# Fewer, larger loads of q and k for the first and the last batch of a fused attention and adapter kernel

## The chip, the cores and the metric

The kernel runs on one core of a Trainium2 chip. The metric is the device time of one execution in microseconds; the median of the runs is given. Times inside the kernel come from the profile of one execution and count from the start of its span.

## The reference

Four batches of 6400 rows of 256 columns. Attention here is between columns (a 256 x 256 matrix for each batch), and its output goes through a mixture of adapters, two of eight for each row.

```python
qn = q / (np.linalg.norm(q, axis=1, keepdims=True) + 1e-06)
kn = k / (np.linalg.norm(k, axis=1, keepdims=True) + 1e-06)
s = kn.transpose(0, 2, 1) @ qn / tau          # per batch 256 x 256, summed over all 6400 rows
s = s - s.max(-1, keepdims=True)
a = np.exp(s); a /= a.sum(-1, keepdims=True) + 1e-09
x = (v @ a).reshape(B * N, 256)
...
logits = x @ w_gate                            # 8 experts, the two largest
for e in range(E):                             # rows that chose e, with their softmax weight w
    z = x[mask] @ A[e]                         # 256 x 16
    delta[mask] += w[mask, k, None] * (z @ B[e])
return x + delta
```

All inputs and the output are float32. q, k, v and the output are 26.2 MB each.

## The kernel before

Each batch is cut into 50 chunks; a chunk of q, k or v is 128 rows of 256 columns, one row on each partition, and a row of the file lies so that consecutive chunks are consecutive in memory for a partition. One chunk is 128 KB in float32 and is turned into bf16 by the load itself. A load of n chunks is therefore 128 runs of n KB.

q and k of a batch go to one buffer, `qk`, of 50 chunks each. There is only one, so a chunk of the next batch may be written only after the same chunk of this batch has been read by PE (`gram`, L259, and `norm`, L270 or L276) and by the engine that squares it (`square`, L251 on ACT, L253 on DVE). v has two buffers, each for one of the three pieces of a batch; v of the last batch goes to `qk`, which is free by then.

For a batch, `gram` adds k^T q over the 50 chunks in PSUM, and `norm` adds the squares through a matrix of ones. The chain of small steps `chain0` to `chain6` makes the softmax and the products with the gate and with A. After that the chunks of v are taken in pairs, one pair to a slot of a long software pipeline: transposes on PE (L409), gate logits for a group of five pairs (L431), z (L517), its transpose (L541), y (L533 and L553), and a copy of the finished pair to the ring `ys` (L557). Batch 0 is read by a loop of its own, two chunks a turn, with squares on DVE and ACT in turn. It runs as far as the loads let it. Batches 1 to 3 are spread over the slots by `GRAM`: batch 1 in slots 8 to 22, batch 2 in 26 to 46, batch 3 in 50 to 68; slot s carries pair s of v.

The stores of finished groups are put off (`DEFER`, `send`): the first goes out late, several groups are sent as one later on, and the last ones are small and issued by SP (L561).

All loads but the first stand in one list, `LOADS`, and are issued by POOL in that order. "q1.13-26" is q of batch 1, chunks 13 to 25. `load_more` is called at each turn of the loop and at each slot: it issues from the list until it comes to a piece whose place in the buffer is still to be read by instructions not yet written. The chunks 0 to 3 of batch 0 are loaded by SP in float32 and cast by DVE and ACT. The three calls `load_more(6)`, `load_more(2)` and `load_more(5)` at the start set how many pieces go out ahead of the constants that POOL makes (`ident`, `ident_f`). The same list order is then the order in which the pieces stand in the queue; an issue waits on POOL for its buffer, and all that stand behind it in the list wait with it.

Of the kernel before, what the change touches and what calls it, by code (L numbers as in the profile page):

```python
# [16 lines left out]
def kernel(  # L17
# [30 lines left out]
    VB, YB = 2, 10  # L48

    VP = [[18, 16, 16]] * 3 + [[26, 24]]  # L50
    LOADS = """q0.4-13 k0.4-13 q0.13-26 k0.13-26 q0.26-38 k0.26-38 q0.38-50 k0.38-50 v0.0-18
        q1.0-13 k1.0-13 v0.18-34 q1.13-26 k1.13-26 q1.26-50 k1.26-38 v0.34-50 k1.38-50
        q2.0-13 k2.0-13 v1.0-18 q2.13-32 k2.13-32 v1.18-34 q2.32-50 k2.32-50 v1.34-50
        q3.0-19 k3.0-19 v2.0-18 q3.19-38 k3.19-38 v2.18-34 q3.38-50 k3.38-50 v2.34-50
        v3.0-26 v3.26-50"""
    SPLIT = {(1, 1): (15, 100, 7), (1, 2): (7, 108, 13)}
    ENDS = 4
# [43 lines left out]
    loads = []  # L101
    for x in LOADS.split():
        c0, c1 = x[3:].split("-")
# [7 lines left out]
    def v_piece(b, c):  # L111
        s = 0
        while c >= VP[b][s]:
            c -= VP[b][s]
            s += 1
        return s, c
# [7 lines left out]
    def load_by_rows(dst, src, m, parts):  # L124

        nc.gpsimd.dma_start(dst[:, ENDS:m - ENDS, :], src[:, ENDS:m - ENDS, :])
        r = 0
        for n in parts:
            nc.gpsimd.dma_start(two_ends(dst, m)[r:r + n], two_ends(src, m)[r:r + n])
            r += n  # L130
        if r < P:
            for c in (0, m - ENDS):
                nc.gpsimd.dma_start(dst[r:P, c:c + ENDS, :], src[r:P, c:c + ENDS, :])

    def load_more(limit=1000):

        while limit and at_load[0] < len(loads):
            kind, b, c0, c1 = loads[at_load[0]]
            if kind in "qk":
                if b > 0 and done[b - 1] < c1:  # L140
                    return
                w, src = (0, q_v) if kind == "q" else (1, k_v)
                nc.gpsimd.dma_start(qk[:, w, c0:c1, :], src[b, :, c0:c1, :])  # L143
            else:
                s, _ = v_piece(b, c0)
                if b == B - 1:

                    if done[b] < c1 or now[0] < HOLD.get(s, 0):
                        return
                    t = qk[:, 0, c0:c1, :]  # L150
                    if s in HOLD:

                        nc.gpsimd.tensor_copy(t[0:1, 0, 0:1], pr[now[0] - 1]["vT"][0:1, 0, 0, 0:1])
                else:
                    n = len(left)
                    if n >= VB and left[n - VB]:
                        return
                    left.append(c1 - c0)
                    t = v_pool.tile([P, max(VP[0]), C], BF16, tag="v", name="vt")[:, 0:c1 - c0, :]
                tiles[b, s] = t  # L160
                if (b, s) in SPLIT:
                    load_by_rows(t, v_v[b, :, c0:c1, :], c1 - c0, SPLIT[b, s])
                else:
                    nc.gpsimd.dma_start(t, v_v[b, :, c0:c1, :])
            at_load[0] += 1
            limit -= 1
# [13 lines left out]

    DL = E * C // P
    nc.sync.dma_start(ast, moe_A.rearrange("e (h l) r -> (e h) (l r)", l=DL))
    load_more(6)
    ones_bf = const.tile([P, P], BF16)
    nc.vector.memset(ones_bf, 1.0)
    ones_f = const.tile([P, P], FP32)
# [3 lines left out]
    for c in range(0, FIRST, 2):  # L190
        nc.vector.tensor_copy(qk[:, 0, c:c + 2, :], stage[:, 0, c:c + 2, :])
        nc.scalar.copy(qk[:, 1, c:c + 2, :], stage[:, 1, c:c + 2, :])
    load_more(2)
    ident = const.tile([P, P], BF16)
    make_identity(nc, ident)
    ident_f = const.tile([P, P], FP32)
# [531 lines left out]
```

## Time and profile before

| | |
|---|---|
| median of 3 runs | 254.01 us (253.96 to 254.12) |
| profiled execution | 254.09 us, its span 252.3 us |
| granted TensorE clock, mean | 0.970 |
| busy share: PE, PE weight loads, DVE, ACT, POOL | 87%, 76%, 61%, 70%, 11% |
| moved to and from HBM | 78.91 MB read, 26.21 MB written, 417 GB/s over the span |
| packets on POOL's queue | 6368, 38.80 MB as written in bf16 |

The busy shares are means over a span with several stages. The stores are issued between 157.8 and 245.8 us; until then the DMA engines carry loads alone. The time from a load's issue to its landing, which the profile gives for each form of load, holds the wait behind the loads ahead of it.

### The profile page before, as it was taken

What the parts mean: (1) busy time and instruction counts of PE and PEld (TensorE: products, weight loads), DVE (VectorE), ACT (ScalarE), POOL (GpSimd) and SP (SyncE); (2) the same over time, 40 slices, a digit from 0 to 9 for tenths busy, and PEclk for the clock granted to TensorE, in tenths of its full rate; (3) what the DMA queues carried; (4) which work ended last, traced back from release to release, by engine and by line L of the source; (5) the groups of instructions that cost most, each with busy time, mean ns of one, the idle gap of its engine ahead of it and who ended that gap; (6) DMA issues with size and microseconds to landing.
All of it is one profiled execution on the core that took longest, in us unless ns stands there. A gap on an engine that the chain in (4) does not pass through costs nothing.

```text
span 252.3 us, 7396 instructions
## 1 busy us (share of the span) xinstructions
PE 219.3 (87%) x3122; PEld 190.8 (76%) x3122; DVE 154.8 (61%) x580; ACT 177.1 (70%) x294; POOL 27.0 (11%) x55
## 2 busy tenths in 40 slices
PE   0478769569999999999999999999999799999980
PEld 0235545347899988989999889899998699999960
DVE  2216513665657578766776877858577767877840
ACT  3315532665798979788888798798878568877870
POOL 8202101010102014105020020010001000000000
PEclk9999989997999999999999999999999899999996
DMA  7999999999999999999999999999999999999996
GB/s 215 220 221 216 217 218 214 212 213 232 203 218 214 214 222 218 203 221 209 212 219 220 216 214 214 257 272 281 269 285 427 303 308 433 411 439 410 424 417 260
DMA packets 9857, 66.80 MB, mean 265 GB/s; under 512 B 1504, under 2 KB 1760, under 8 KB 5856
## 3 DMA queue, kind: packets, MB, share of 16 engines
q0 software_dynamic: 6368, 38.80, 74.2%
q10 hardware_dynamic: 1872, 23.59, 22.2%
q1 hardware_dynamic: 1584, 3.94, 4.3%
q8 instruction: 24, 0.39, 0.6%
q14 instruction: 9, 0.07, 0.1%
HBM read 78.91 MB, written 26.21 MB: 417 GB/s over the span
## 4 chain that ended last, share of the span: by engine, by line
PE 54%; DMA 34%; DVE 5%; ACT 1%; issue 1%; POOL 1%; DVEq 0%; ACTq 0%; POOLq 0%
DMA qk<-in_k_dram 34%; PE y_ps L533 15%; PE acc L259 9%; PE zg L517 7%; PE y_ps L553 7%; PE vT_ps L409 6%; PE zg L541 4%; PE nrm L276 3%; PE vT_ps L431 3%; POOL qk L143 1%; DVE gz L521 1%; ACT sq L251 1%; DVE lg L455 0%; PE nrm L318 0%; ACT ys L557 0%
## 5 line engine op out<-in xcount | busy, mean ns | idle before, releaser
L251 ACT ACTIVATE sq<-qk 128x1024 bf16<-128x1024 bf16 x87 | 89.6, 1055 | 23.4 <-DMA qk<-in_k_dram 16.3
L259 PE MATMUL acc<-qk 128*128 128x256 bf16 x400 | 73.3, 284 | 16.4 <-DMA qk<-in_k_dram 10.1
L557 ACT COPY ys<-y_ps 128x512 f32<-128x512 f32 x100 | 58.7, 587 | 18.2 <-PE y_ps L553 16.4
L533 PE MATMUL y_ps<-ae,vT 128*128 128x256 bf16 x400 | 60.3, 273 | 0.0
L259 PEld LDWEIGHTS <-qk 128*128 128x128 bf16 x400 | 33.9, 101 | 26.7 <-DMA qk<-in_k_dram 12.0
L521 DVE TENSOR_TENSOR gz<-zg,gate 128x256 bf16<-128x256 f32 x100 | 41.7, 418 | 14.3 <-PE zg L517 12.7
L276 PEld LDWEIGHTS <-sq 128*128 128x128 bf16 x600 | 35.9, 97 | 7.6 <-ACT sq L251 4.0
L517 PE MATMUL zg<-wa_sb,vT 128*128 128x128 bf16 x400 | 38.8, 220 | 1.2 <-DVE gzT L547 1.2
L420 DVE COPY vT<-vT_ps 128x512 bf16<-128x512 bf16 x60 | 25.4, 423 | 22.5 <-PE vT_ps L409 21.3
L553 PE MATMUL y_ps<-ball_sb,gzT 128*128 128x256 bf16 x200 | 38.4, 274 | 0.0
L276 PE MATMUL nrm<-ones_bf,sq 128*128 128x1 bf16 x600 | 35.5, 164 | 2.4 <-ACT sq L251 2.1
L533 PEld LDWEIGHTS <-vT 128*128 128x128 bf16 x400 | 33.5, 97 | 2.6
L418 ACT COPY vT<-vT_ps 128x512 bf16<-128x512 bf16 x40 | 23.5, 587 | 13.2 <-PE vT_ps L409 11.7
L409 PE MATMUL vT_ps<-ident,vt 128*128 128x128 bf16 x300 | 29.0, 220 | 1.8 <-DVE vT L420 1.5
L517 PEld LDWEIGHTS <-vT 128*128 128x128 bf16 x400 | 26.5, 98 | 3.3 <-issue 1.9
L541 PE MATMUL zg<-ident,gz 128*128 128x128 bf16 x200 | 27.8, 221 | 1.2 <-DVE gz L521 0.8
L409 PEld LDWEIGHTS <-vt 128*128 128x128 bf16 x300 | 22.5, 98 | 4.1 <-issue 2.0
L547 DVE COPY gzT<-zg 128x256 bf16<-128x256 bf16 x90 | 25.2, 280 | 0.0
L253 DVE TENSOR_TENSOR sq<-qk 128x1024 bf16<-128x1024 bf16 x13 | 9.0, 692 | 23.9 <-DMA qk<-in_k_dram 15.9
L541 PEld LDWEIGHTS <-gz 128*128 128x128 bf16 x200 | 15.1, 98 | 2.7 <-DVE gz L521 2.4
L553 PEld LDWEIGHTS <-gzT 128*128 128x128 bf16 x200 | 16.2, 98 | 0.4
L270 PE MATMUL nrm<-sq,ones_bf 128*128 128x512 bf16 x50 | 16.4, 419 | 0.0
(77 smaller groups left out, 189.2 us busy)
## 6 DMA issues: line engine op xcount, KB each, us to landing
out_dram<-ys ACTq DMA_DIRECT2D x9, 1280.0 KB, 13.0
out_dram<-ys ACTq DMA_DIRECT2D x3, 2560.0 KB, 19.4
vt<-in_v_dram POOLq DMA_DIRECT2D x4, 1024.0 KB, 21.0
qk<-in_k_dram POOLq DMA_DIRECT2D x5, 768.0 KB, 28.1
out_dram<-ys ACTq DMA_DIRECT2D x1, 3840.0 KB, 22.8
qk<-in_q_dram POOLq DMA_DIRECT2D x3, 1216.0 KB, 20.1
qk<-in_k_dram POOLq DMA_DIRECT2D x3, 1216.0 KB, 25.4
vt<-in_v_dram POOLq DMA_DIRECT2D x3, 1152.0 KB, 18.2
```

The costliest lines, as they stand in the source:

```text
L251: nc.scalar.activation(sq, src, ACT.Square)
L259: nc.tensor.matmul(acc[b][:, ic, :], qk[:, 1, c, ic * P:(ic + 1) * P], qk[:, 0, c, :], start=(c == 0 and ic == 0), stop=(c == NC - 1), ski ...
L276: nc.tensor.matmul(nrm[b][:, j:j + 1], sq[:, w, c % 2, ic * P:(ic + 1) * P], ones_bf[:, 0:1], start=(c == 0 and j == 0), stop=(c == NC - 1 ...
L409: nc.tensor.matmul(pt[:, ic, sc * P:(sc + 1) * P], vt[:, o + sc, ic * P:(ic + 1) * P], ident, is_transpose=True, start=(i == 0), stop=(i = ...
L420: nc.vector.tensor_copy(dst, src)
L517: nc.tensor.matmul(z[:, sc, :], r["vT"][:, ic, sc, :], st[b]["wa"][:, ic, E:E + ER], start=(sc == 0 and ic == 0), stop=(sc == 1 and ic == ...
L521: nc.vector.tensor_tensor(out=gz.rearrange("p c (e r) -> p c e r", e=E), in0=z.rearrange("p c (e r) -> p c e r", e=E), in1=gr["gate"][:, r ...
L533: nc.tensor.matmul(y[:, sc, :], r["vT"][:, ic, sc, :], st[b]["a"][:, ic, :], start=(sc == 0 and ic == 0), stop=False, skip_group_check=True)
L541: nc.tensor.matmul(gt[:, sc, :], r["gz"][:, sc, :], ident, is_transpose=True, start=(sc == 0), stop=(sc == 1))
L547: nc.vector.tensor_copy(gzT, gt)
L553: nc.tensor.matmul(r["y"][:, sc, :], r["gzT"][:, sc, :], ball_sb, start=False, stop=(sc == 1), skip_group_check=True)
L557: nc.scalar.copy(gr["ys"][:, r["w"]:r["w"] + 2, :], r["y"])
```

## The change

Two lines of `LOADS` change, and two of the limits at the start.

Batch 0: q and k came in four pieces each (chunks 4 to 12, 13 to 25, 26 to 37, 38 to 49), q and k in turn. Now q comes in two (4 to 25, 26 to 49) and k in three (4 to 25, 26 to 36, 37 to 49). The first call issues four pieces where it issued six, the second one where it issued two; so the constants on POOL still follow the whole of batch 0's list.

Batch 3: q and k came in three pieces of 19, 19 and 12 chunks. Now q comes in two of 19 and 31, and k in three of 19, 15 and 16. The places of v's pieces between them stay: one after the first q and k, one after the second, one after the last k.

```diff
-    LOADS = """q0.4-13 k0.4-13 q0.13-26 k0.13-26 q0.26-38 k0.26-38 q0.38-50 k0.38-50 v0.0-18
+    LOADS = """q0.4-26 k0.4-26 q0.26-50 k0.26-37 k0.37-50 v0.0-18
         q1.0-13 k1.0-13 v0.18-34 q1.13-26 k1.13-26 q1.26-50 k1.26-38 v0.34-50 k1.38-50
         q2.0-13 k2.0-13 v1.0-18 q2.13-32 k2.13-32 v1.18-34 q2.32-50 k2.32-50 v1.34-50
-        q3.0-19 k3.0-19 v2.0-18 q3.19-38 k3.19-38 v2.18-34 q3.38-50 k3.38-50 v2.34-50
+        q3.0-19 k3.0-19 v2.0-18 q3.19-50 k3.19-34 v2.18-34 k3.34-50 v2.34-50
         v3.0-26 v3.26-50"""
...
-    load_more(6)
+    load_more(4)
...
-    load_more(2)
+    load_more(1)
```

## The prediction

> **What bounds the kernel now.** I read the page's slices first, then the chain, then the queue of loads row by row.
>
> ```profile
> DMA  7999999999999999999999999999999999999996
> ...
> PE 54%; DMA 34%; DVE 5%; ACT 1%; issue 1%; POOL 1%; DVEq 0%; ACTq 0%; POOLq 0%
> ```
>
> The two lines seem to disagree. The chain gives PE over half of the span, but the chain follows one last instruction back; it does not say what else was full. The slices do: the 16 DMA engines are busy in 38 of 40 slices at nine tenths or more, loads first and stores after. The kernel must move all of q, k, v and the output, and there is no slice in which the transfers wait for the compute. So I take DMA work as the bound of the whole span, and PE as a second chain that has to stay ahead of its due times. Two places show how they hang together:
>
> ```profile
> 27.48 34.30 DMA qk<-in_k_dram
> 61.88 1.06 ACT sq L251
> ...
> 78.89 27.81 DMA qk<-in_k_dram
> ```
>
> These are steps of the chain: start, length. A load of batch 1 issued at 27.48 lands at 61.78, one of batch 2 issued at 78.89 lands at 106.70. Some 30 us between issue and landing is queue, not transfer: the loads stand in line. Compute waits there for bytes, so whatever PE loses earlier is given back at these points, as long as the line itself never runs empty.
>
> At the end of the span the same question is how much the last store has to spare:
>
> ```profile
> out_dram<-ys SPq DMA_DIRECT2D x3, 256.0 KB, 5.6
> ...
> ys<-in_q_dram SPq DMA_DIRECT2D x1, 512.0 KB, 3.6
> ```
>
> The last stores of 256 KB take 5.6 us from issue to landing; at the start, with empty queues, a transfer of twice the size from the same issuer took 3.6 us. So at least 2.0 us of the 5.6 is line. PE could finish 2 us later and the last byte would land when it does now.
>
> **What a load costs besides its bytes.** The change takes out three loads in batch 0 (eight to five) and one in batch 3 (six q and k pieces to five), with the same bytes. Four issues in a row give the price, since each lands when the one ahead of it has landed and its own bytes have passed:
>
> ```profile
> 42.67 0.53 POOL L143 DMA_DIRECT2D qk<-in_q_dram  x1 [14.66 <-PE acc L259]
> 43.19 0.54 POOL L143 DMA_DIRECT2D qk<-in_k_dram  x1
> 52.70 0.53 POOL L164 DMA_DIRECT2D vt<-in_v_dram  x1 [8.98 <-PE vT_ps L409]
> 53.22 0.54 POOL L143 DMA_DIRECT2D qk<-in_k_dram  x1
> ```
>
> ```profile
> qk<-in_q_dram POOLq DMA_DIRECT2D x1, 1536.0 KB, 26.4
> qk<-in_k_dram POOLq DMA_DIRECT2D x2, 768.0 KB, 28.8
> vt<-in_v_dram POOLq DMA_DIRECT2D x1, 1024.0 KB, 24.9
> ```
>
> The second fence is of the DMA issues in that stretch, with KB each and time to landing. The 24 chunks of q (1536 KB) land at 42.67 + 26.4 = 69.07, which is 7.29 after the 61.78 above. The 16 chunks of v land at 77.60. The two 12-chunk loads of k, by their median 28.8, land in the mean at (43.19 + 53.22) / 2 + 28.8 = 77.0, and the loads ahead of them in the mean at (69.07 + 77.60) / 2 = 73.34, so a 12-chunk load takes 3.67. The slope is (7.29 - 3.67) / 12 = 0.302 us per chunk, and 3.67 - 12 x 0.302 = 0.05 us is left for the load itself. The rows are rounded to 0.1 us, so the bounds are 0 and 0.1. Four loads fewer: 0 to 0.4 us of DMA work, and I take 4 x 0.05 = 0.2 us, all of it on the bound.
>
> The Trainium skill says otherwise: "DMA: Bandwidth & Descriptors", section "Anatomy of one DMA — SWDGE (gpsimd) path", puts a fixed part of about 2.0 us on each DMA of this kind, so four loads would be worth 8 us. Here the trace disagrees for loads that stand in line: the next one's bytes flow while the fixed part passes, and 0.05 us is what is left.
>
> The POOL time of the four issues (0.53 to 0.54 each, rows above) is worth nothing: POOL waits 14.66 us ahead of one of them.
>
> **Batch 0: a later start.** Chunks 4 to 12 now come with chunk 25, not ahead.
>
> ```profile
> 19.93 0.39 PE L259 MATMUL acc<-qk 128*128 128x256 bf16 x2 [2.72 <-DMA qk<-in_k_dram]
> 20.16 0.59 PE L270 MATMUL nrm<-sq,ones_bf 128*128 128x512 bf16 x2
> 20.59 0.60 PE L259 MATMUL acc<-qk 128*128 128x256 bf16 x4
> 21.03 0.59 PE L270 MATMUL nrm<-sq,ones_bf 128*128 128x512 bf16 x2
> ...
> 35.51 0.92 PE L259 MATMUL acc<-qk 128*128 128x256 bf16 x4 [1.99 <-DMA qk<-in_k_dram]
> ...
> 41.97 1.46 PE L270 MATMUL nrm<-sq,ones_bf 128*128 128x512 bf16 x6
> ```
>
> ```profile
> 53.45 5.77 ACT L251 ACTIVATE sq<-qk 128x1024 bf16<-128x1024 bf16 x6
> ...
> 158.28 2.00 ACT L251 ACTIVATE sq<-qk 128x1024 bf16<-128x1024 bf16 x2
> ...
> 173.11 1.99 ACT L251 ACTIVATE sq<-qk 128x1024 bf16<-128x1024 bf16 x2
> ```
>
> In the first fence (PE in order of time) the waits end with landings: k's chunks up to 25 are there at 19.9, the last ones at 35.5. The same bytes stand ahead of both in the new order, so these two instants stay. A pair of chunks takes 20.16 to 21.03 = 0.87 us. The last run, 12 chunks from 35.51, took until 43.43: less six pairs (5.2) and the four closing norms (two pairs' worth, 0.87) that leaves 1.8 us, the price of starting after an idle stretch.
>
> New: chunks 4 to 25 are 11 pairs from 19.9, 9.6 us and 1.8 for the start, to 31.3. Chunks 26 to 36 have landed by then: 19.9 + 35 x 0.302 = 30.5. Five pairs to 35.6, and now PE meets the last piece at 35.5 without a gap, so the 1.8 isn't paid again. Seven pairs, 6.1, the sixteen matmuls for moe_A, which ran in the old gap (16 x 128 columns, a pair has 4 x 256 + 2 x 512, so 0.87), and the closing norms, 0.87: 43.4. Batch 0 ends where it ended. It may be a microsecond off either way, and that is covered: ACT's first six squares of batch 1 end at 59.22, and their successor waits until 61.88 for bytes, 2.7 us. Without that cover it would cost what it is late.
>
> The queue does not run empty meanwhile: q of batch 1 may follow once chunk 13 is read, about five pairs and the 1.8 after 19.9, near 26; batch 0's loads last until 35.5.
>
> **Batch 3: fewer, later.** q's second piece now reaches to chunk 50 and overwrites the last chunk of batch 2, so POOL's issue waits for PE's last gram of it, where it had gone out at 131; k's second piece queues behind it.
>
> ```profile
> 131.60 0.56 POOL L143 DMA_DIRECT2D qk<-in_k_dram  x1
> 145.23 0.53 POOL L164 DMA_DIRECT2D vt<-in_v_dram  x1 [13.07 <-PE y_ps L553]
> 145.75 0.55 POOL L143 DMA_DIRECT2D qk<-in_q_dram  x1
> 146.27 0.56 POOL L143 DMA_DIRECT2D qk<-in_k_dram  x1
> ```
>
> ```profile
> qk<-in_k_dram POOLq DMA_DIRECT2D x1, 1216.0 KB, 25.4
> ...
> qk<-in_k_dram POOLq DMA_DIRECT2D x1, 768.0 KB, 26.8
> ```
>
> ```profile
> 140.38 0.38 PE L259 MATMUL acc<-qk 128*128 128x256 bf16 x2
> ...
> 167.36 0.39 PE L409 MATMUL vT_ps<-ident,vt 128*128 128x128 bf16 x4
> ```
>
> Old: k's chunks 19 to 37 land at 131.60 + 25.4 = 157.0, the 38 chunks of the two second pieces took 38 x 0.302 + 0.1 = 11.6, so v's piece ahead of them was through at 145.4. New: q's 31 chunks can go out at 140.38 + 0.38 = 140.8, 4.6 us before that. POOL sits in that wait; behind it stand k's second piece, at once, and v's load, which goes out at 145.23 as before because its buffer is free then.
>
> Due times: k's second piece ends after 46 chunks, 145.4 + 46 x 0.302 + 0.1 = 159.4. Its first reader is the square of chunks 18 and 19, the second of the two at 158.28, so at 159.3: level. v's middle piece follows, 16 chunks: 164.3 if alone; at the mean pace from 157.0 to 173.07 (146.27 + 26.8; 40 chunks, 0.40 each, stores between them) 157.0 + 24 x 0.40 = 166.6. It is first read at 167.36: on time by 0.8 to 3. k's last piece ends with the same byte as before, 173.1; chunk 34 is squared at 174.1, the second of the two at 173.11. On time by 1. A miss of some tenths at any of the three falls into the 2.0 us of the end. Cost: 0.
>
> **Sum.** The profiled execution took 254.09 us, the span 252.3 and 1.8 around it. 254.09 - 0.2 = 253.9; the median is 0.08 below the profiled run, so 253.8.
>
> **Rivals.** Faster, by a latency that does not hide: SP's first load took 3.6 us, of which its four chunks' bytes are 1.2, so 2.4 us is latency at both ends. If each load held the queue for that long, four fewer would give 254.0 - 9.6 = 244.4. (By the price that the Trainium skill's "DMA: Bandwidth & Descriptors" gives, 246.0.) The four landings above speak against it; 2 in 100. A smaller gain of that sort, beyond 0.5 us, would need over 0.12 us per load, just above the bound; 12 in 100.
>
> Slower, by a hole in the queue: between 131 and 140.8 POOL has nothing to issue. If q's late piece arrives after v's bytes are through, the engines stand idle and DMA work, the bound, moves back one for one. With SP's 2.4 us of latency, bytes issued for at 140.8 flow by 143.2 at the latest; v's last ones, landing at 145.4, have passed by 145.4 - 2.4 = 143.0 at the earliest. Against it: even these worst ends leave a hole of 0.2 us. For it: no row shows a POOL load entering an empty queue. The point from which it decides is a latency of 2.7 us (143.0 + 0.5 - 140.8); one of 3.4, a microsecond above the row, gives up to 253.8 + 1.0 = 254.8. 20 in 100.
>
> Slower, by PE: the start in batch 0 costs over 2.7 us more than worked out, or the three due times of batch 3 are missed by more than 2.0 us together. 255, for a miss of 3; 5 in 100.
>
> No effect at all, because the 0.05 us is rounding: 254.0. It goes with the forecast; together 61 in 100.
>
> **Numbers.** About 0.2% (0.5 us) is what a measurement of this kernel can tell from no change. Forecast and no effect, 253.6 to 254.1, are within it: 0.61. Faster 0.02 + 0.12 = 0.14. Slower 0.20 + 0.05 = 0.25. The range reaches from a gain of 0.7 (the 0.4 bound and 0.3 of run scatter and doubt) to the hole's 254.8 and 0.1 of scatter: 253.3 to 254.9.
>
> **What would show it.** Right: DMA slices full as before; PE idle from 8 to 20 and then without a gap until about 43.4; the wait at 61.9 still there; the landing at 106.7 earlier by 0.1 to 0.2; q's late piece issued near 140.8, no dip in the DMA share from 142 to 145; the squares near 159.3 and 174.1 without a wait of a microsecond. Wrong: a dip there, batch 0 ending past 46, a store at the end that lands in under 4 us (the end is then PE's), or a chunk that takes other than 0.30 us in the bigger loads.

## The result, and the profile after

| | before | after |
|---|---|---|
| median | 253.99 us (253.84 to 254.14, 6 runs) | 255.59 us (255.33 to 256.04, 6 runs) |
| profiled execution, its span | 254.09 us, 252.3 us | 255.68 us, 253.9 us |
| ratio | | 1.0064, 95% interval 1.0051 to 1.0077 |

The change costs 1.6 us. The forecast was 253.8 in a range up to 254.9, with 25 in 100 for a slower kernel, 20 of them for a hole in the queue. The page of after first: the DMA slices, and the chain's shares by engine.

```profile
DMA  7999999999999999999999999999999999999994
...
PE 63%; DMA 18%; DVE 10%; ACT 3%; issue 2%; POOL 0%; DVEq 0%; ACTq 0%; POOLq 0%
```

The slices are as full as before; only the last one is thinner (4 for 6). The chain moved towards PE, which would mislead if it were read alone, because PE and ACT are done earlier than in the kernel before. The last copy of outputs on ACT, in order of time, of before and of after:

```profile
244.56 1.24 ACT L557 COPY ys<-y_ps 128x512 f32<-128x512 f32 x2 [0.24 <-PE y_ps L553]
```

```profile
244.05 1.24 ACT L557 COPY ys<-y_ps 128x512 f32<-128x512 f32 x2 [0.24 <-PE y_ps L553]
```

Compute ends 0.5 us earlier and the span 1.6 us later. The DMA issues of after say the same: the last 256 KB stores, 5.6 us from issue to landing before, now stand in a longer line.

```profile
out_dram<-ys SPq DMA_DIRECT2D x3, 256.0 KB, 7.7
```

How much work is left at the end, and on how many of the 16 engines? The windows of one microsecond from 248 on (the last two columns are the DMA share and GB/s), of before:

```profile
248.00:249.00 1.00, 0.00 (x0) 0.00 (x0) 0.00 (x0) 0.00 (x0) 0.00 (x0) 0.50 1.03 401
249.00:250.00 1.00, 0.00 (x0) 0.00 (x0) 0.00 (x0) 0.00 (x0) 0.00 (x0) 0.50 0.83 320
250.00:251.00 1.00, 0.00 (x0) 0.00 (x0) 0.00 (x0) 0.00 (x0) 0.00 (x0) 0.50 0.23 88
```

and of after:

```profile
248.00:249.00 1.00, 0.00 (x0) 0.00 (x0) 0.00 (x0) 0.00 (x0) 0.00 (x0) 0.50 0.99 393
249.00:250.00 1.00, 0.00 (x0) 0.00 (x0) 0.00 (x0) 0.00 (x0) 0.00 (x0) 0.50 0.92 358
250.00:251.00 1.00, 0.00 (x0) 0.00 (x0) 0.00 (x0) 0.00 (x0) 0.00 (x0) 0.50 0.55 213
251.00:252.00 1.00, 0.00 (x0) 0.00 (x0) 0.00 (x0) 0.00 (x0) 0.00 (x0) 0.50 0.16 61
252.00:253.00 1.00, 0.00 (x0) 0.00 (x0) 0.00 (x0) 0.00 (x0) 0.00 (x0) 0.50 0.03 12
```

The shares add up to 2.09 and 2.65 us: the DMA engines as a whole are 0.56 us late. But the last bytes are 1.6 us later, since few engines are still at work by then (0.03 of 16 is half of one engine over a microsecond). A mean loss of 0.56 became 1.6 at the end because the slowest engine ends the span.

Where were the 0.56 us lost? The traces record every packet: a load has 128 of them, one for each partition, and on each engine it ends with a packet of 4 bytes. I counted the packets of both traces, each load's packet at the float32 bytes that it reads (twice what it writes, which is what the GB/s of the views count), and divided the difference in bytes moved by 428 GB/s, a rate that slices near the end of after's page reach:

| us from the start | after is behind before by |
|---|---|
| 142 | -0.06 us |
| 145 | 0.20 |
| 158 | 0.16 |
| 164 | 0.61 |
| 249 | 0.55 |

There are two places. In the first, q's late piece goes out. POOL in order of time, after:

```profile
130.28 0.53 POOL L164 DMA_DIRECT2D vt<-in_v_dram  x1 [13.16 <-PE y_ps L553]
141.02 0.53 POOL L143 DMA_DIRECT2D qk<-in_q_dram  x1 [10.21 <-ACT ed L480]
141.81 0.53 POOL L143 DMA_DIRECT2D qk<-in_k_dram  x1 [0.26 <-issue]
```

It was issued at 141.02, and by the packet records its first packet started at 142.62. The time in which engines stood idle here (fewer than 16 packets under way) is only 0.07 us as a mean of the 16. Another 0.17 us is in q's first packets: seven took 1.28 to 2.10 us where its others took 1.19. The kernel before has no such idle time, and neither has any kernel below that comes within 0.2% of it. The second place lies at 158 to 164, where the first output is stored. Windows of before, then of after:

```profile
140.00:146.00 6.00, 5.89 (x78) 5.13 (x77) 5.12 (x23) 4.77 (x13) 0.77 (x2) 1.00 1.02 215
146.00:158.00 12.00, 11.91 (x211) 10.94 (x209) 9.12 (x35) 11.04 (x19) 0.82 (x2) 1.00 1.03 216
158.00:164.00 6.00, 5.91 (x96) 5.37 (x93) 4.84 (x21) 4.57 (x8) 0.00 (x0) 1.00 1.01 256
```

```profile
140.00:146.00 6.00, 5.80 (x80) 5.05 (x78) 4.96 (x22) 4.96 (x13) 2.02 (x4) 1.00 1.04 215
146.00:158.00 12.00, 11.91 (x213) 10.95 (x210) 9.10 (x34) 11.05 (x18) 0.10 (x1) 1.00 1.00 212
158.00:164.00 6.00, 5.80 (x91) 5.26 (x88) 4.88 (x20) 4.57 (x8) 0.00 (x0) 1.00 1.00 230
```

The share is 1.01 and 1.00 in the last rows, but 230 GB/s pass instead of 256. A share counts the time in which a packet is under way, a stalled one too; the bytes tell whether it moves. In this stretch 28 of after's packets of v's middle piece took 0.70 to 1.08 us where most took 0.63, and none of before's did. The first slow ones start at 159.7, after the store's issue (157.6) and ahead of its first packet (161.2), so the store's bytes alone can't be what holds them up.

### The profile page after: what moved, and what is told of

Its sections match the earlier page's. It is cut to its first block, busy times and chain, and to the rows that moved or that the text cites. A ratio compares the mean times of both kernels' runs of the same rounds, so it can differ in the third digit from the quotient of the medians.

```text
span 253.9 us, 7388 instructions
## 1 busy us (share of the span) xinstructions
PE 217.4 (86%) x3122; PEld 190.1 (75%) x3122; DVE 154.7 (61%) x580; ACT 177.1 (70%) x294; POOL 24.7 (10%) x51
## 4 chain that ended last, share of the span: by engine, by line
PE 63%; DMA 18%; DVE 10%; ACT 3%; issue 2%; POOL 0%; DVEq 0%; ACTq 0%; POOLq 0%
DMA qk<-in_k_dram 18%; PE acc L259 14%; PE y_ps L533 13%; PE zg L517 7%; PE y_ps L553 6%; PE vT_ps L409 6%; PE nrm L270 5%; PE zg L541 4%; PE nrm L276 4%; PE vT_ps L431 3%; DVE gz L521 2%; ACT sq L251 2%; ACT ys L557 1%; PE nrm L318 1%; DVE e L463 1%
## 5 line engine op out<-in xcount | busy, mean ns | idle before, releaser
L533 PEld LDWEIGHTS <-vT 128*128 128x128 bf16 x400 | 33.3, 97 | 2.5
L517 PEld LDWEIGHTS <-vT 128*128 128x128 bf16 x400 | 26.1, 97 | 3.1 <-issue 1.8
```

Source lines behind the costliest of these rows:

```text
L517: nc.tensor.matmul(z[:, sc, :], r["vT"][:, ic, sc, :], st[b]["wa"][:, ic, E:E + ER], start=(sc == 0 and ic == 0), stop=(sc == 1 and ic == ...
L533: nc.tensor.matmul(y[:, sc, :], r["vT"][:, ic, sc, :], st[b]["a"][:, ic, :], start=(sc == 0 and ic == 0), stop=False, skip_group_check=True)
```

## The experiments

Theory 1: the wait of q's second piece for the end of batch 2 lets the queue of loads run dry. Its rivals: batch 0's later start; k's other pieces; the wait itself as something that harms in another way than by an empty queue. The before beside each run had medians of 254.02 to 254.08.

**Each half alone.** Batch 0's line and limits with batch 3 as before, then the reverse:

```diff
-    LOADS = """q0.4-13 k0.4-13 q0.13-26 k0.13-26 q0.26-38 k0.26-38 q0.38-50 k0.38-50 v0.0-18
+    LOADS = """q0.4-26 k0.4-26 q0.26-50 k0.26-37 k0.37-50 v0.0-18
```

> Batch 0's five loads alone; batch 3 as in the kernel before. Theory 1 (the loss is a hole in the load queue in batch 3): as before or 0.1 to 0.2 us faster, 253.8 to 254.0, PE's batch 0 ending a microsecond later without effect. Rival theory (the late start of batch 0 costs the end): about 255.5, like the whole change.

Measured: 253.98 us (253.73 to 254.09, 11 runs), ratio 0.9993 (0.9983 to 1.0003). Batch 0's part costs nothing, and gains nothing that shows.

```diff
-        q3.0-19 k3.0-19 v2.0-18 q3.19-38 k3.19-38 v2.18-34 q3.38-50 k3.38-50 v2.34-50
+        q3.0-19 k3.0-19 v2.0-18 q3.19-50 k3.19-34 v2.18-34 k3.34-50 v2.34-50
```

> Batch 3's five q and k loads alone; batch 0 as before. Theory 1: 255.3 to 255.9, the whole loss, with a dip of the DMA rate from 142 to 144.5 and the slow packets near 161. Rival (batch 0): 254.0.

Measured: 255.94 us (255.77 to 256.07, 5 runs), ratio 1.0069 (1.0051 to 1.0088). The whole loss is in this line. Here the first place shows in the windows too, since q went out later still (141.62). A window counts a packet whole where it starts, so the first two rows are to be read together: 196 GB/s from 142 to 146, where before has 212.

```profile
142.00:144.00 2.00, 1.89 (x22) 1.55 (x20) 1.79 (x10) 1.58 (x4) 0.68 (x2) 1.00 1.23 229
144.00:146.00 2.00, 2.00 (x25) 1.69 (x24) 1.35 (x4) 1.91 (x5) 0.45 (x1) 1.00 0.77 163
...
158.00:164.00 6.00, 6.00 (x107) 5.63 (x106) 4.83 (x20) 4.72 (x7) 0.00 (x0) 1.00 1.01 227
```

**The same wait with cover.** The whole change, with k's second piece listed ahead of q's:

```diff
-        q3.0-19 k3.0-19 v2.0-18 q3.19-50 k3.19-34 v2.18-34 k3.34-50 v2.34-50
+        q3.0-19 k3.0-19 v2.0-18 k3.19-34 q3.19-50 v2.18-34 k3.34-50 v2.34-50
```

> The whole change, but k3.19-34 stands ahead of q3.19-50 in the list, so POOL can issue it near 131 and the queue has 15 chunks (4.6 us) more when q's late piece is issued near 141. Bytes, sizes and the number of loads are those of the change. Theory 1: no dip at 142 to 144.5, 253.7 to 254.2. Rival theory 2 (the slow packets near 161, where v's middle piece meets the first store, are a loss of their own): dip at 142 gone, dip at 161 stays, 254.5 to 255.2.

Measured: 253.94 us (253.71 to 254.11, 11 runs), ratio 0.9993 (0.9983 to 1.0003). POOL in order of time, and the window of the second place:

```profile
130.16 0.53 POOL L164 DMA_DIRECT2D vt<-in_v_dram  x1 [13.21 <-PE y_ps L553]
130.68 0.55 POOL L143 DMA_DIRECT2D qk<-in_k_dram  x1
140.90 0.53 POOL L143 DMA_DIRECT2D qk<-in_q_dram  x1 [9.68 <-PE zg L517]
```

```profile
158.00:164.00 6.00, 5.80 (x91) 5.29 (x90) 4.76 (x20) 4.57 (x7) 0.00 (x0) 1.00 1.00 259
```

The same 31 chunks of q go out at the same time (140.90 against 141.02) after a wait of the same length. The difference is that 960 KB of k stand in the queue meanwhile, ahead of q. The 1.6 us are gone, and so is the second dip. This parts Theory 1 from the wait as such.

**The parts of batch 3's line.** First k's new pieces alone (q as before), then q's merge alone (k as before):

```diff
+        q3.0-19 k3.0-19 v2.0-18 q3.19-38 k3.19-34 v2.18-34 q3.38-50 k3.34-50 v2.34-50
```

> Batch 0 as before; batch 3 with q in 19, 19, 12 as before and only k in 19, 15, 16. No load waits for the end of batch 2. Theory 1: 253.9 to 254.2, no dip. Theory 2 (slow packets where v's middle piece meets the first store): v's piece lands some 1.2 us earlier than before, so it hardly meets the store: 254.0. Third theory (the finer k pieces are late for batch 3): over 254.5 with waits of ACT's squares on k.

Measured: 254.06 us (253.89 to 254.34, 11 runs), ratio 0.9997 (0.9987 to 1.0007). Nothing.

```diff
+        q3.0-19 k3.0-19 v2.0-18 q3.19-50 k3.19-38 v2.18-34 k3.38-50 v2.34-50
```

> Batch 0 as before, k of batch 3 in 19, 19, 12 as before, only q's last two pieces merged to 31 chunks: one load fewer, and both second pieces wait for the end of batch 2. Theory 1 (the hole in the queue behind this wait is the whole loss): 255.5 to 256.1, as batch 3's part alone. Rival (the finer and later k pieces carry part of it): 254.5 to 255.2.

Measured: 255.78 us (255.37 to 256.58, 6 runs), ratio 1.0071 (1.0059 to 1.0084). All of it.

**How early is early enough?** The whole change, with q's piece ended at chunk 49 or 47 and the rest loaded after v's piece, so that the wait ends sooner:

```diff
+        q3.0-19 k3.0-19 v2.0-18 q3.19-49 k3.19-34 v2.18-34 q3.49-50 k3.34-50 v2.34-50
...
+        q3.0-19 k3.0-19 v2.0-18 q3.19-47 k3.19-34 v2.18-34 q3.47-50 k3.34-50 v2.34-50
```

> The whole change, but q's late piece ends at chunk 49 and the last chunk comes as a load of its own after v's middle piece, so the late piece waits for one chunk less of batch 2 and is issued about 1.4 us earlier, near 139.6; one load more. Theory 1: the hole is mostly gone, since the first engines run out near 142: 253.9 to 254.5. Rival (any wait for batch 2's end is too late, as the store's first bytes take 3.5 us from the issue): over 255.

> As the last one, with q's late piece ending at chunk 47: issued about 3 us earlier than in the change, near 138. Theory 1: no hole, 253.8 to 254.1. If it is still over 254.5, the loss is not the wait but the size or the order of the pieces.

Their issues of q on POOL:

```profile
139.75 0.53 POOL L143 DMA_DIRECT2D qk<-in_q_dram  x1 [9.01 <-ACT sq L251]
```

```profile
138.12 0.53 POOL L143 DMA_DIRECT2D qk<-in_q_dram  x1 [7.13 <-ACT sq L251]
```

Measured: to 49, 254.21 us (253.81 to 255.76, 11 runs), ratio 1.0015 (1.0003 to 1.0027); to 47, 253.89 us (253.66 to 254.03, 11 runs), ratio 0.9993 (0.9984 to 1.0001). With the kernels above that is a row of doses: issue at 138.12, no loss; at 139.75, the edge, with runs on both sides; at 141.02 to 141.62, 1.6 to 1.9 us. From the edge, an issue 1.3 us later turns a loss of 0.2 in the median into the whole loss. The trace of the edge is of an execution that took 254.00: in it q's first packet (141.98) follows at once on v's last one on that engine (141.96). Of its slower executions there is no trace, so that a hole cost them time is not shown.

**A bigger saving of loads.** If a load costs 0.05 us, eight fewer should show. v's two later pieces of batch 1 are each issued in several parts by rows; here in one load each, on top of the kernel with k ahead of q:

```diff
-    SPLIT = {(1, 1): (15, 100, 7), (1, 2): (7, 108, 13)}
+    SPLIT = {}
```

> The reordered version (k3.19-34 ahead of q3.19-50), and v's two pieces of batch 1 that were loaded in six and four transfers by rows are loaded in one each: eight loads fewer. If a load costs 0.05 us on every engine and small runs move slower: 253.2 to 253.7. If the split evens out the engines and the slowest one sets the end: 254.0 or above.

Measured: 254.25 us (254.09 to 254.58, 11 runs), ratio 1.0008 (0.9999 to 1.0017). The gain did not come. By the packet records this kernel was 0.39 us ahead of before at 140 and 0.30 behind at 200. The window, of this kernel and of before:

```profile
180.00:200.00 20.00, 18.34 (x299) 16.72 (x296) 14.61 (x60) 15.67 (x32) 0.70 (x2) 1.00 1.01 317
```

```profile
180.00:200.00 20.00, 18.17 (x293) 16.59 (x292) 14.62 (x60) 15.42 (x32) 0.72 (x2) 0.99 1.01 325
```

What the fewer loads gained was lost again at 180 to 200; why there, these runs don't show. The time is that of the second expectation, but whether the parts by rows even out the engines was not measured.

**The second dip.** Is it the first store's? First with the stores put off by one group more in the changed kernel (`DEFER` 9 for 8):

> The whole change with the stores put off by one group of pairs more (DEFER 9 for 8), so the first store is issued some 10 us later than 157.6. The first hole, at 142 to 144.5, stays. Theory 2a (the slow packets near 161 come where the first store meets loads whose engines have lost their lead): the rate from 158 to 164 is that of loads alone, about 215, with no slow packets, and the dip, if it comes, comes some 10 us later. Theory 2b (the dip near 161 belongs to the loads alone, at a fixed distance behind the first hole): the rate from 158 to 164 falls below 205. Time: 254.5 to 256.

Measured: 272.14 us (271.6 to 273.22, 4 runs), ratio 1.0724 (1.0702 to 1.0747). The time is of no use: the ring holds ten groups, and copies to it now wait for stores (first fence, the waits: us in total, times, longest). But the window without a store tells something (second fence).

```profile
ACT ys L557 <- DMA out_dram<-ys: 18.7, 3, 13.5
```

```profile
158.00:164.00 6.00, 5.80 (x91) 5.29 (x89) 4.81 (x20) 4.57 (x8) 0.00 (x0) 1.00 1.04 217
```

217 GB/s is the full rate of loads alone (216 for before at 146 to 158), though q went out at 140.85 and by the packet records the first place was there (0.17 us behind at 158, 0.11 at 164). In this window a single packet of v's piece was slow (0.81 us). From 166.8 on packets of the loads are slow again, up to 1.28 us: a few ahead of the later store's issue (167.65), most around its first bytes (171.05). The engines move 190 GB/s from 168 to 172, less than with loads alone, so here too the dip lies near the store. Then the reverse, one group earlier, for both kernels (`DEFER` 7 for 8):

> The changed kernel, but with the first group of outputs sent one group earlier, so about 11 us before the 157.6 us of the changed kernel. Theory 2a, the second dip belongs to the first store meeting a load queue that the first hole has left uneven: the dip moves with the store, 158 to 164 us moves 250 GB/s or more, and the dip is now near the store. Theory 2b, the dip belongs to the loads that stand in the queue at 160: it stays, 158 to 164 us at 235 GB/s or less. Time by both, if the first hole stays the cause: 1.0 to 2.0 us above the run with the loads of before and the same earlier store.

> The kernel before with the first group of outputs sent one group earlier, the control for the run above. Both theories: no hole, no dip, since the load queue is never drained; all bytes the same, so 253.8 to 254.6 us. If the dip near the first store is there as well, it is the store's alone and the first hole has no part in it.

Measured: changed kernel 256.82 us (256.54 to 258.88, 4 runs), before 254.37 us (254.22 to 254.45, 10 runs). They send the first group at 145.5 and 145.3. Windows of the changed kernel with the earlier store, then of before with it:

```profile
146.00:158.00 12.00, 11.91 (x202) 10.93 (x200) 9.12 (x36) 11.17 (x18) 0.60 (x2) 1.00 0.98 240
158.00:164.00 6.00, 3.60 (x69) 3.19 (x68) 2.94 (x12) 1.68 (x3) 0.00 (x0) 0.96 1.03 264
```

```profile
146.00:158.00 12.00, 11.91 (x208) 10.94 (x206) 9.12 (x35) 11.05 (x19) 0.94 (x2) 1.00 1.02 268
158.00:164.00 6.00, 6.00 (x101) 5.48 (x98) 4.83 (x21) 4.63 (x7) 0.00 (x0) 1.00 1.04 258
```

The dip moved with the store: 240 against 268 GB/s at 146 to 158, and none at 158 to 164. Before, with the same early store and no empty queue, has no dip. So in these kernels it takes both: a queue that has run dry, and the first store after it. In bytes, counted as above, the changed kernel is 0.27 us behind its control at 146 and 1.02 at 158: this dip took 0.75 us where after's took 0.45, so it is larger where the store follows the hole more closely. The difference in time, 2.45 us, is above the 1.0 to 2.0 expected, but it is not the dip's alone: k's second piece lands at 163.7 here, PE is busy for only 3.60 of the 6 us from 158, and the last copy of outputs ends at 248.9 where the control's ends at 246.0. What makes the loads' packets slow in the dip is open.

No kernel here clearly beats the kernel before: k ahead of q (253.94 us) and q to chunk 47 (253.89) undo the loss and are within 0.1% of before.

## Why the prediction was wrong

**The bound: right.** DMA work sets the end. The last copy of outputs ended 0.5 us earlier and that bought nothing.

**0.05 us per load: of the right order, and of no use.** Three loads fewer put the kernel with batch 0's part alone 0.08 us ahead in bytes at 142, where 0.15 was worked out; eight fewer, in the kernel without row parts, gave 0.26 by 140 (0.39, less the 0.13 of the kernel it is made from), where 0.4 would have been due: 0.03 us per load. The prediction's bounds of 0 to 0.1 were narrower than its rows allow: the 0.05 is a difference in which landings rounded to 0.1 us enter several times, and rounding alone can move it by 0.25 us. No median fell by the gain in bytes. Here the forecast counted a gain of mean DMA work as a gain at the end.

**Batch 0: right in kind, the start mis-sized, and covered as worked out.** PE in order of time, after:

```profile
19.77 1.03 PE L259 MATMUL acc<-qk 128*128 128x256 bf16 x4 [11.30 <-DMA qk<-in_k_dram]
20.59 1.06 PE L270 MATMUL nrm<-sq,ones_bf 128*128 128x512 bf16 x2
21.44 1.06 PE L259 MATMUL acc<-qk 128*128 128x256 bf16 x4
22.30 1.06 PE L270 MATMUL nrm<-sq,ones_bf 128*128 128x512 bf16 x2
...
42.98 1.46 PE L270 MATMUL nrm<-sq,ones_bf 128*128 128x512 bf16 x6
```

The first pairs take 1.71 us (20.59 to 22.30), about twice the 0.87. The batch ends at 44.44 where 43.4 was worked out: 23 pairs at 0.87, moe_A and the norms make 21.8 of the 24.7 from 19.77, so the start cost 2.9, not 1.8. The cover of 2.7 us took the extra microsecond, and the wait it was to come from is still there, 1.58 us of it. ACT in order of time:

```profile
61.81 1.06 ACT L251 ACTIVATE sq<-qk 128x1024 bf16<-128x1024 bf16 x1 [1.58 <-DMA qk<-in_k_dram]
...
159.40 1.06 ACT L251 ACTIVATE sq<-qk 128x1024 bf16<-128x1024 bf16 x1 [0.24 <-DMA qk<-in_k_dram]
...
174.13 2.00 ACT L251 ACTIVATE sq<-qk 128x1024 bf16<-128x1024 bf16 x2
```

**Batch 3's due times: right, to 0.3 us.** The squares at 159.4 and 174.1 stand where they stood. The DMA issues, with KB and time to landing:

```profile
qk<-in_q_dram POOLq DMA_DIRECT2D x1, 1984.0 KB, 13.7
...
vt<-in_v_dram POOLq DMA_DIRECT2D x1, 1024.0 KB, 21.5
qk<-in_k_dram POOLq DMA_DIRECT2D x1, 1024.0 KB, 27.8
qk<-in_k_dram POOLq DMA_DIRECT2D x1, 960.0 KB, 17.5
```

k's second piece lands at 141.81 + 17.5 = 159.3 (159.4 was worked out), v's at 145.04 + 21.5 = 166.5 (166.6), k's last at 145.56 + 27.8 = 173.4 (173.1), q at 141.02 + 13.7 = 154.7.

**The step that failed: "143.0 at the earliest".** The hole was a rival with 20 in 100, its mechanism and place were right, and its bounds were wrong. The prediction took the queue as one line that empties at one instant, the landing of v's piece less 2.4 us. A landing is that of the last of 16 engines. In the changed kernel v's piece ends on the first engine at 142.0 and on the last at 144.7 (by the packets of 4 bytes), 2.7 us apart; in all kernels here it is 2.5 to 3.1. So a load issued at 141.02, whose first packet came 1.6 us later, was too late for the first three engines and in time for the last, and every landing stayed where it was while bytes were lost ahead of it. The latency, which was the doubt stated, was below the 2.4 allowed; in the other kernels with a hole it was 1.2 to 1.4 from issue to first packet. The Trainium skill's "DMA: Bandwidth & Descriptors", section "Anatomy of one DMA — SWDGE (gpsimd) path", puts most of its fixed part of about 2.0 us behind the last byte. This trace has it the other way round: 1.6 us ahead of q's first packet, and 0.4 from v's last packet (144.7) to its landing (130.28 + 14.8 = 145.1).

The prediction also said that no row shows a POOL load entering an empty queue. One of before comes near it:

```profile
qk<-in_q_dram POOLq DMA_DIRECT2D x1, 576.0 KB, 7.1
```

These are POOL's first nine chunks of q, issued at 1.23 while loads of SP were under way on the same engines. Their bytes take 2.7 us (9 x 0.302), which leaves 4.4, more than the 2.7 from which the rival was to decide. It isn't the latency that was met at 141, but it spoke for a higher chance.

**The price: "one for one".** The hole itself took 0.26 us (-0.06 to 0.20 in the table), near the 0.2 of the rival's worst ends, and most of that was slow packets, not idle engines. The rest was priced nowhere: 0.45 us more at the first store (0.16 to 0.61 in the table), and a step from 0.56 in the mean to 1.6 at the slowest engine.

**The sign named.** "No dip in the DMA share from 142 to 145" was to show the forecast right, and the share has none (1.04 at 140 to 146). It was the wrong column: a stalled packet counts as busy for as long as it takes.

## What to carry to other kernels

A load that must wait for a buffer needs bytes standing in the queue behind which it can arrive: count from the issue to the moment at which the first engine runs out, not the last, and put a piece that is free to go ahead of the one that waits. In this kernel a quarter of a microsecond lost in the queue that bounds the span became 1.6 at the end, since the slowest engine sets the end; don't price such a loss one for one. Landings that stay on time don't show that the queue stayed full, and neither does the DMA share. The packets around the wait, the bytes per window behind it and the thinning of the last microseconds do.

## What was not expected of the hardware

- The 16 engines of one queue finish the same load 2.5 to 3.1 us apart (v's piece ahead of the hole, in every kernel here; 142.0 to 144.7 in after).
- The first packets of a load that meets a dry queue are slow: seven took 1.28 to 2.10 us where the others took 1.19, and that cost more than the idle time (0.17 against 0.07 us).
- The first store after a dry queue costs load bandwidth (230 against 256 GB/s, 240 against 268 with an earlier store), and not without the dry queue.
- Eight loads fewer on a full queue gained 0.26 us by 140 and lost more than that by 200.
